# Position bias: the coefficient matrices written by GpSimd in quarters of partitions, and the first pair's operands loaded and split in the first groups

## Chip, cores and metric

The program runs on one core of one Trainium2 chip. The metric is the time of one execution in microseconds (us). The profile has one execution more, with its span (first to last instruction) beside its own time.

## The reference

Attention with a learned position bias feeds a chain of dense layers, and that feeds a top-1 mixture of 8 experts. Only the bias and the scores matter for this change:

```
B, H, S, D = 4, 8, 576, 64;  hidden = 32
rel = |i - j|;  psi_rel = log1p(rel);  psi_i = log1p(max(i, 1))
x    = psi_rel / psi_i                            # (S, S)
h    = relu(x * w1 + b1)                          # (S, S, 32)
bias = h @ w2                                     # (S, S, 8), one for each head
scores = q @ k.T / sqrt(D) + bias;  attn = softmax(scores);  out = attn @ v
x = (B*S, H*D) of out
x = ((x @ w1m) * (x @ w2m)) @ w3m @ w_out         # dense layers
result = top-1 of 8 experts, relu(x @ w1e) @ w2e, gated
```

## The kernel before

The program has four stages: `p0` (position bias, about the first 147 us), `p1` (attention, 16 pairs of a head and two batches), `p2` (dense layers) and `p3` (experts). An order of the instructions is written out by hand; each engine executes its own in that order, and so does the queue of the DMA issues on SyncE.

`p0` turns the bias into a matrix product. A hidden unit's relu of x is a step function of the row times something linear in log1p of the distance. The 576 distances are cut into 9 groups (`gg`) of 64; a group has 16 slots of 4 distances. The 128 partitions hold 4 distances x 32 hidden units. For each slot a mask of 128 x 576 is made (`mask`, L263 on VectorE, L261 on ScalarE): partition (distance g, unit u) and column i say if the unit is on in row i. The masks of group `gg + 1` are made while the matmuls of group `gg` run. For each group and each of up to five tiles `t` of rows (order 0, 4, 3, 1, 2; tile 4 has 64 rows) L345 multiplies the 16 masks by the matrix `mv`, 48 matmuls.

`mv` (two buffers, group `gg` uses `mvs[gg % 2]`) has the shape [128, 3, 16, 2, 8, 4]: three bf16 parts of a coefficient, slot, a = 0 for the linear or a = 1 for the constant coefficient, head, distance g. It is zero but where the partition's quarter (its 32 partitions) equals g. `split3` (L152, L154, GpSimd) cuts coefficients into three bf16 parts; `place` (L161, VectorE) multiplies them by the 0/1 matrix `bkb` of quarters and so writes zeros and values in one go, three operations of 128 x 512 elements. The constant coefficients (a = 1, `c3`) are placed once in each buffer, the linear ones (a = 0, from `coefs`) for each group. `coefs(gg + 2)` is called when group `gg` starts, and its `place` runs at the start of group `gg + 1`.

After a tile's matmuls `evac` scales one half of the result on ScalarE (L268) and adds the other on VectorE (L279, into `ds`). After each odd group `flush` writes the finished 128 distances to the DRAM tensor `dsym` (L221) and their mirror image, which GpSimd copies in reverse order into `md` (L235, three buffers), by L238. The attention stage reads the bias from `dsym` with `load_nb` (L382, L385).

In the same stage 24 blocks of weights are loaded as 64-bit floats (`load`, L180, five buffers) and converted (`begin`, `conv`: L89 on ScalarE, L91 to L93 on VectorE, L202 on ScalarE, L207 on VectorE), and products of these weights are made on TensorE (`wp_mm`, L245). The steps of a group are sorted by a key between 0 and 1 (`mixed`) and dealt out over its tiles. At each tile's end `ahead` takes a task of preparation for the attention stage from a list: `first` (constants, a clear, the loads of q, k and v of the first pair by L390, L391, L393), ten steps that split them (L403 to L423, on ScalarE and GpSimd), the loads of the second pair's q and k, and a small split of the gate weights. It does so from the fourth group on (`gg > 2`), not at a group's first tile.

Of the kernel before, what the change touches and what calls it, by code (L numbers as in the profile page):

```python
# [11 lines left out]
BF16 = mybir.dt.bfloat16  # L12
# [3 lines left out]
ALU = mybir.AluOpType  # L16
# [4 lines left out]
B, H, S, D = 4, 8, 576, 64  # L21
# [5 lines left out]
P = 128  # L27
# [43 lines left out]
class Kern:  # L71
# [4 lines left out]
    def T(self, pool, shape, dt, tag, **k):  # L76
        self.n += 1
        return pool.tile(shape, dt, name=f"{tag}_{self.n}", tag=tag, **k)
# [18 lines left out]
    def p0(self, dsym, wp_dram, late, ahead=lambda gg, ti: None):  # L97
# [3 lines left out]
        with ExitStack() as es:  # L101
# [14 lines left out]
            w1c, b1c, w2r = small[:, 0:1], small[:, 1:2], small[:, 2:2 + H]  # L116
            ivp, blk = ivb[:, 0:5], ivb[:, 5:9]
            mvs = [T(c, [P, 3, 16, 2, H, 4], BF16, f"mv{r}") for r in range(2)]
            th = T(c, [P, 144], F32, "th")
            tS = T(c, [P, 144], F32, "tS")  # L120
            sm = T(c, [P, 4], F32, "sm")
# [23 lines left out]

            def split3(src, n, sub):

                p3 = T(st, [P, 3, n, H], BF16, f"p3{sub}")
                rest = T(st, [P, n, H], F32, f"rest{sub}", bufs=1)
                for k in range(3):  # L150
                    v_ = src if k == 0 else rest
                    gp.tensor_scalar(out=p3[:, k], in0=v_, scalar1=1.0, scalar2=1.0, op0=ALU.mult, op1=ALU.mult)  # L152
                    if k < 2:
                        gp.tensor_tensor(out=rest, in0=v_, in1=p3[:, k], op=ALU.subtract)  # L154
                return p3

            def place(r, a, p3):

                src = p3 if p3.shape[2] == 16 else p3.to_broadcast([P, 3, 16, H])
                for k in range(3):  # L160
                    v.tensor_tensor(out=mvs[r][:, k, :, a], in0=src[:, k].unsqueeze(3).to_broadcast([P, 16, H, 4]),  # L161
                                    in1=bkb.unsqueeze(1).unsqueeze(1).to_broadcast([P, 16, H, 4]), op=ALU.mult)

            def coefs(gg):
                al = T(st, [P, 16, H], F32, "al", bufs=1)
                gp.tensor_tensor(
                    out=al, in0=cf[:, 0:1, :].to_broadcast([P, 16, H]),
                    in1=L4[:, 16 * gg:16 * gg + 16].unsqueeze(2).to_broadcast([P, 16, H]), op=ALU.mult)
                a3 = split3(al, 16, "a")
                return lambda: place(gg % 2, 0, a3)  # L170

            wf = T(late.xp, [P, KD * NT], F32R, "xT")
            woh, wol = (wf[:, KF * DM * n:KF * DM * (n + 1)].rearrange("p (k d) -> p k d", k=KF) for n in range(2))
# [2 lines left out]
            def load(i, b):  # L176
                raws[i, b] = T(st, [P, DM, 2], I32, "w3", bufs=NRAW)
                src = I["w_out"][:, 2 * i:2 * i + 2, :] if i < 4 else I["w3t"][i - 4]
                src = src.rearrange("p k d -> p (k d)")[:, DM * b:DM * b + DM]
                nc.sync.dma_start(out=raws[i, b].rearrange("p n t -> p (n t)"), in_=src.bitcast(I32))  # L180
# [103 lines left out]
            order = list(CV)  # L284
            for _ in range(NRAW):
                load(*order.pop(0))
            begin(0)
            c3 = split3(cf[:, 1:2, :], 1, "c")
            pl = coefs(0)
            for q in range(0, 16, 4):  # L290
                for k in range(3):
                    mask(0, q + k)
                mask(0, q + 3, True)
                if q == 0:
                    place(0, 1, c3)
                if q == 4:
                    pl()
            pl = coefs(1)
            prev = None
            st_ = {}  # L300
            for gg in range(9):
                ts = [t for t in (0, 4, 3, 1, 2) if 64 * gg < DMAX[t]]
                wph = list(range(WPH[gg], WPH[gg + 1]))
                bg, bga = [], []
                if gg < 8:
                    for q in range(16):
                        act = (q + 1) * NACT // 16 > q * NACT // 16
                        (bga if act else bg).append(lambda q=q, act=act: mask(gg + 1, q, act))

                cs = []  # L310
                n = CONV[gg + 1] - CONV[gg]
                for x, c_ in enumerate(range(CONV[gg], CONV[gg + 1])):

                    cs += [((x + 0.1 + 0.2 * k) / n, (c_, k)) for k in range(4)]
                    if c_:
                        cs.append(((x + 0.9) / n, (c_ - 1, 4)))
                if gg == 8:
                    cs.append((1, (len(CV) - 1, 4)))

                def cstep(n, k):  # L320
                    if k == 0:
                        begin(n + 1)
                        st_[n] = conv(*CV[n])
                    st_[n][k]()

                items = [(FM * (k + 0.5) / len(bg), x) for k, x in enumerate(bg)]
                items += [(k, lambda x=x: cstep(*x)) for k, x in cs]
                if gg < 8:
                    items.append((0, pl))
                    if gg == 0:  # L330
                        items.append((0, lambda: place(1, 1, c3)))
                    if gg < 7:
                        pl = coefs(gg + 2)
                mixed = [x for _, x in sorted(items, key=lambda x: x[0])]
                nt = len(ts)
                for ti, t in enumerate(ts):
                    for x in wph[len(wph) * ti // nt:len(wph) * (ti + 1) // nt]:
                        wp_mm(x // KF, x % KF)
                    n = 64 if t == 4 else P
                    pb = T(ps, [P, 2, 2, H, 8, 4], F32, "pb")  # L340
                    mv = mvs[gg % 2]
                    for s in range(16):
                        m_ = mss[gg, s // 8]
                        for k in range(3):
                            nc.tensor.matmul(out=pb[:n, s // 8, :, :, s % 8], lhsT=m_[:, s % 8, P * t:P * t + n], rhs=mv[:, k, s], start=(k == 0), stop=(k == 2))  # L345
                    fin = evac(*prev) if prev else None
                    for x in bga[len(bga) * ti // (nt - 1):len(bga) * (ti + 1) // (nt - 1)]:
                        x()
                    m0, m1 = len(mixed) * ti // nt, len(mixed) * (ti + 1) // nt
                    for x in mixed[m0:m1]:  # L350
                        x()
                    if fin:
                        fin()
                    ahead(gg, ti)
                    prev = (gg, t, pb)
# [1032 lines left out]
def build(tc, I, out):  # L1388
    K = Kern(tc, I, out)
    nc = tc.nc  # L1390
    with tc.manual_schedule(), ExitStack() as es:
# [18 lines left out]
            nc.gpsimd.memset(pre.qs[0].bitcast(F32), 0.0)  # L1410
            pre.load(0)

        tasks = [first, lambda: None] + [lambda x=x: x[0](*x[1:]) for x in pre.split(0)]
        tasks += [lambda: pre.load(1, v=False), lambda: wgs.append(K.wg_stack(c, cst["wg"]))]

        def ahead(gg, ti):
            if gg > 2 and ti and tasks:
                tasks.pop(0)()
            if ti == 1 and gg > 5:
                pre.load_nb(0, (8 - gg, ) if gg < 8 else (3,))  # L1420

# [120 lines left out]
```

## Time and profile before

| what | us |
|---|---|
| median of 3 runs | 1056.01 (1052.99 to 1056.57) |
| the profiled execution's own time | 1054.81 |
| its span | 1052.9 |
| TensorE busy | 979.5 (93%) |
| VectorE busy | 770.6 (73%) |
| ScalarE busy | 679.3 (65%) |
| GpSimd busy | 400.9 (38%) |

The shares are means over four stages that have different limits. For a change in the first stage, the busy times of that stage and the chain of waits in it say more. In the rows PE is TensorE's matmul, PEld its weight load, DVE VectorE, ACT ScalarE, POOL GpSimd, SPq the DMA queue of SyncE; L161 is line 161 of the kernel. PEclk is the share of full speed that TensorE's clock was granted.

### The profile page before, as it was taken

How to read it: one execution, taken by the hardware profiler on the slowest of the kernel's cores; microseconds unless marked ns; L12 is line 12 of the kernel's file. 1: busy time of each engine (PE TensorE's matmuls, PEld its weight loads, DVE VectorE, ACT ScalarE, POOL GpSimd, SP SyncE). 2: the span in 40 equal slices, each digit the busy share in tenths (PEclk: the TensorE clock that was granted, in tenths of full speed). 3: DMA queues.
4: the chain of work that ended last, by engine and by line, in shares of the span. 5: the costliest groups of instructions: out<-in, count | busy, mean ns of one | idle time of the engine just before them, and what ended most of it. 6: DMA issues, size and time to landing. Idle time of an engine off the chain costs nothing.

```text
span 1052.9 us, 21995 instructions
## 1 busy us (share of the span) xinstructions
PE 979.5 (93%) x8134; PEld 906.2 (86%) x8134; DVE 770.6 (73%) x1426; ACT 679.3 (65%) x1304; POOL 400.9 (38%) x468
## 2 busy tenths in 40 slices
PE   3588989999999999799999999999979999999996
PEld 3577778999999999699999999999978888888885
DVE  8997977999999998799321232123497999989996
ACT  5787758999999999344322222122226888888885
POOL 4255518899999986444100000000052121111111
PEclk9899989999999999889999999999989999999999
DMA  4599984453434422243000000000423326411173
GB/s 133 137 247 234 254 242 152 128 172 121 158 96 143 159 72 67 82 149 111 21 21 21 11 11 21 21 21 1 134 87 120 118 78 216 155 41 40 44 277 109
DMA packets 62419, 116.54 MB, mean 111 GB/s; under 512 B 14495, under 2 KB 33567, under 8 KB 62048
## 3 DMA queue, kind: packets, MB, share of 16 engines
q1 hardware_dynamic: 58496, 104.14, 32.0%
q0 software_dynamic: 3520, 10.75, 3.0%
q8 instruction: 67, 1.10, 0.4%
q14 instruction: 48, 0.39, 0.1%
q10 hardware_dynamic: 288, 0.15, 0.1%
HBM read 155.68 MB, written 25.15 MB: 172 GB/s over the span
## 4 chain that ended last, share of the span: by engine, by line
PE 43%; DVE 21%; issue 18%; DMA 12%; ACT 5%; POOL 0%; SPq 0%; POOLq 0%; DVEq 0%; ACTq 0%
PE ab L712 17%; DMA out<-or,sci 9%; PE o L781 8%; PE pv L569 6%; PE sc L485 4%; PE tr L541 3%; DVE etl L558 2%; DVE t L492 2%; DVE mv L161 2%; PE pv L245 2%; DVE mask L263 2%; DMA dsym<-ds 1%; ACT e L501 1%; DVE ds L279 1%; DVE qs L410 1%
## 5 line engine op out<-in xcount | busy, mean ns | idle before, releaser
L758 DVE TENSOR_TENSOR g<-ab,asb 128x256 f32<-128x256 f32 x72 | 30.4, 423 | 143.3 <-ACT asb L757 143.1
L512 POOL TENSOR_SCALAR e<-e,su 128x576 f32<-128x576 f32 x144 | 108.8, 760 | 27.2 <-DVE su L508 14.2
L492 DVE CUSTOM_DVE_ANT_0 t<-sc,nb 128x576 f32<-128x576 f32 x144 | 108.0, 750 | 11.4 <-PE sc L485 10.0
L501 ACT ACTIVATE e<-t,mn 128x576 f32<-128x576 f32 x144 | 112.2, 779 | 4.3 <-DVE mn L492 2.8
L558 DVE TENSOR_TENSOR etl<-tr,eth 128x512 fp32r<-128x512 f32 x144 | 98.9, 687 | 15.8 <-ACT eth L549 12.3
L345 PEld LDWEIGHTS <-mask 128*128 128x128 bf16 (+1 forms) x1872 | 67.1, 108 | 47.3 <-issue 36.2
L345 PE MATMUL pb<-mv,mask 128*128 128x64 bf16 (+1 forms) x1872 | 71.1, 203 | 38.8 <-DVE ds L279 22.2
L1328 POOL DMA_INDIRECT out<-or,sci x21 | 24.9, 1184 | 200.2 <-ACT or L1327 190.5
L485 PE MATMUL sc<-kh,qs 128*128 128x288 f32 x320 | 96.5, 318 | 3.3 <-DVE ds L279 3.3
L712 PE MATMUL ab<-xh,wh 128*128 128x256 f32 x576 | 95.6, 289 | 1.3 <-DVE g L758 1.3
L1225 DVE TENSOR_TENSOR w1l<-w1r,w1h 128x1024 fp32r<-128x1024 f32 x80 | 92.6, 1220 | 5.1 <-ACT w1h L1224 5.1
L541 PE MATMUL tr<-k_ident,e 128*128 128x128 f32 x576 | 86.4, 273 | 8.9 <-DVE etl L558 8.9
L1276 DVE TENSOR_TENSOR w2l<-w2r,w2h 128x1024 fp32r<-128x1024 f32 x80 | 92.6, 1220 | 2.7
L953 POOL DMA_INDIRECT xh<-x2r,gi x1 | 1.4, 1352 | 243.8 <-DMA w1r<-in_w1e 243.8
L712 PE MATMUL ab<-xh,wl 128*128 128x256 f32 x576 | 93.8, 286 | 0.0
L712 PE MATMUL ab<-xl,wh 128*128 128x256 f32 x576 | 93.8, 286 | 0.0
L485 PE MATMUL sc<-kl,qs 128*128 128x288 f32 x320 | 90.0, 297 | 0.0
L549 ACT CAST eth<-tr 128x512 fp32r<-128x512 f32 x144 | 82.6, 576 | 2.2 <-PE tr L541 1.4
L712 PEld LDWEIGHTS ab<-xh,wh 128*128 128x128 f32 x576 | 80.9, 195 | 1.7 <-DVE g L758 1.5
L1224 ACT CAST w1h<-w1r 128x1024 fp32r<-128x1024 f32 x84 | 82.1, 1069 | 0.0
L712 PEld LDWEIGHTS ab<-xh,wl 128*128 128x128 f32 x576 | 80.8, 195 | 0.0
L712 PEld LDWEIGHTS ab<-xl,wh 128*128 128x128 f32 x576 | 80.7, 194 | 0.0
(322 smaller groups left out, 2805.7 us busy)
## 6 DMA issues: line engine op xcount, KB each, us to landing
w1r<-in_w1e SPq DMA_DIRECT2D x84, 512.0 KB
w2r<-in_w2e SPq DMA_DIRECT2D x80, 512.0 KB
q<-in_qd SPq DMA_DIRECT2D x16, 576.0 KB
k<-in_kd SPq DMA_DIRECT2D x16, 576.0 KB
w<-in_w3t SPq DMA_DIRECT2D x16, 512.0 KB
raw<-in_w SPq DMA_DIRECT2D x16, 512.0 KB
nb<-dsym SPq DMA_DIRECT2D x7, 1152.0 KB
dsym<-ds SPq DMA_DIRECT2D x14, 512.0 KB
```

Of the source, the lines that this page charges most:

```text
L345: nc.tensor.matmul(out=pb[:n, s // 8, :, :, s % 8], lhsT=m_[:, s % 8, P * t:P * t + n], rhs=mv[:, k, s], start=(k == 0), stop=(k == 2))
L485: nc.tensor.matmul(out=sc[:, f, 0:288], lhsT=l, rhs=r, start=(n == 0), stop=(n == len(lst) - 1))
L492: nc.vector.tensor_tensor_reduce(out=t_.rearrange("p (f k) -> p f k", f=2), in0=sc[:, :, 0:288], in1=pre.nb[h % 2][:, tt, :].rearrange("p ...
L501: nc.scalar.activation(out=e, in_=t_, func=AF.Exp, scale=-1.0, bias=mn, accum_out=su[:, i % 3:i % 3 + 1])
L512: nc.gpsimd.tensor_scalar(out=e, in0=e, scalar1=su[:, i % 3:i % 3 + 1], scalar2=1.0, op0=ALU.mult, op1=ALU.mult)
L541: nc.tensor.transpose(pt[:, kb, :], e[:, P * kb:P * kb + P], ident)
L549: nc.scalar.copy(out=dh, in_=src)
L558: nc.vector.tensor_tensor(out=dl, in0=src, in1=dh.bitcast(F32), op=ALU.subtract)
L712: nc.tensor.matmul(out=p[:, a], lhsT=w[f][:, a, k, :], rhs=x[:, k, :], start=(k == 0 and n == 0), stop=(k == KD - 1 and n == 2))
L781: nc.tensor.matmul(out=o[:, a, 0:c1 - c0], lhsT=g[:, sl], rhs=w[:, f, c0:c1], start=(f == 0 and n == 0), stop=(f == KF - 1 and n == 2))
L1225: eng.tensor_tensor(out=w1l[:, k], in0=w1r[:, k], in1=w1h[:, k].bitcast(F32), op=ALU.subtract)
L1276: nc.vector.tensor_tensor(out=w2l[:, sl], in0=w2r[:, sl], in1=w2h[:, sl].bitcast(F32), op=ALU.subtract)
```

## The change

GpSimd clears both `mv` buffers once at the start. `place` then writes only the nonzero places: for each quarter g an operation on its 32 partitions copies the three parts of 16 slots x 8 heads (384 elements) to the places of that g. It does so on GpSimd, four operations for each group. Only the constant part of the first buffer stays on VectorE, in the old form. `coefs` splits and places in one call; `coefs(gg + 1)` stands at key 0.15 of group `gg`. The first group's masks are made ahead of the first conversion, 10 on VectorE and 6 on ScalarE (before 12 and 4). The list of preparation is cut in two: `first` and the split of the first pair are taken from the first group on, one task at each tile of the first group and two later; the loads of the second pair and the gate weights are taken from the fourth group on.

```diff
@@ -116,6 +116,8 @@
             w1c, b1c, w2r = small[:, 0:1], small[:, 1:2], small[:, 2:2 + H]
             ivp, blk = ivb[:, 0:5], ivb[:, 5:9]
             mvs = [T(c, [P, 3, 16, 2, H, 4], BF16, f"mv{r}") for r in range(2)]
+            for m_ in mvs:
+                nc.gpsimd.memset(m_, 0.0)
             th = T(c, [P, 144], F32, "th")
             tS = T(c, [P, 144], F32, "tS")
             sm = T(c, [P, 4], F32, "sm")
@@ -145,7 +147,7 @@
 
             def split3(src, n, sub):
 
-                p3 = T(st, [P, 3, n, H], BF16, f"p3{sub}")
+                p3 = T(st, [P, 3, n, H], BF16, f"p3{sub}", bufs=1)
                 rest = T(st, [P, n, H], F32, f"rest{sub}", bufs=1)
                 for k in range(3):
                     v_ = src if k == 0 else rest
@@ -156,18 +158,18 @@
 
             def place(r, a, p3):
 
-                src = p3 if p3.shape[2] == 16 else p3.to_broadcast([P, 3, 16, H])
-                for k in range(3):
-                    v.tensor_tensor(out=mvs[r][:, k, :, a], in0=src[:, k].unsqueeze(3).to_broadcast([P, 16, H, 4]),
-                                    in1=bkb.unsqueeze(1).unsqueeze(1).to_broadcast([P, 16, H, 4]), op=ALU.mult)
+                n = p3.shape[2]
+                for g in range(4):
+                    q = slice(32 * g, 32 * g + 32)
+                    src = p3[q] if n == 16 else p3[q].to_broadcast([32, 3, 16, H])
+                    gp.tensor_scalar(out=mvs[r][q, :, :, a, :, g], in0=src, scalar1=1.0, scalar2=1.0, op0=ALU.mult, op1=ALU.mult)
 
             def coefs(gg):
                 al = T(st, [P, 16, H], F32, "al", bufs=1)
                 gp.tensor_tensor(
                     out=al, in0=cf[:, 0:1, :].to_broadcast([P, 16, H]),
                     in1=L4[:, 16 * gg:16 * gg + 16].unsqueeze(2).to_broadcast([P, 16, H]), op=ALU.mult)
-                a3 = split3(al, 16, "a")
-                return lambda: place(gg % 2, 0, a3)
+                place(gg % 2, 0, split3(al, 16, "a"))
 
             wf = T(late.xp, [P, KD * NT], F32R, "xT")
             woh, wol = (wf[:, KF * DM * n:KF * DM * (n + 1)].rearrange("p (k d) -> p k d", k=KF) for n in range(2))
@@ -284,18 +286,16 @@
             order = list(CV)
             for _ in range(NRAW):
                 load(*order.pop(0))
+            c3 = split3(cf[:, 1:2, :], 1, "c")
+            coefs(0)
+            for q in range(16):
+                mask(0, q, q in (2, 5, 7, 10, 13, 15))
+                if q == 4:
+
+                    for k in range(3):
+                        v.tensor_tensor(out=mvs[0][:, k, :, 1], in0=c3[:, k].to_broadcast([P, 16, H]).unsqueeze(3).to_broadcast([P, 16, H, 4]),
+                                        in1=bkb.unsqueeze(1).unsqueeze(1).to_broadcast([P, 16, H, 4]), op=ALU.mult)
             begin(0)
-            c3 = split3(cf[:, 1:2, :], 1, "c")
-            pl = coefs(0)
-            for q in range(0, 16, 4):
-                for k in range(3):
-                    mask(0, q + k)
-                mask(0, q + 3, True)
-                if q == 0:
-                    place(0, 1, c3)
-                if q == 4:
-                    pl()
-            pl = coefs(1)
             prev = None
             st_ = {}
             for gg in range(9):
@@ -325,12 +325,11 @@
 
                 items = [(FM * (k + 0.5) / len(bg), x) for k, x in enumerate(bg)]
                 items += [(k, lambda x=x: cstep(*x)) for k, x in cs]
-                if gg < 8:
-                    items.append((0, pl))
-                    if gg == 0:
-                        items.append((0, lambda: place(1, 1, c3)))
-                    if gg < 7:
-                        pl = coefs(gg + 2)
+                if gg == 0:
+                    coefs(1)
+                    place(1, 1, c3)
+                elif gg < 8:
+                    items.append((0.15, lambda: coefs(gg + 1)))
                 mixed = [x for _, x in sorted(items, key=lambda x: x[0])]
                 nt = len(ts)
                 for ti, t in enumerate(ts):
@@ -1410,12 +1409,16 @@
             nc.gpsimd.memset(pre.qs[0].bitcast(F32), 0.0)
             pre.load(0)
 
-        tasks = [first, lambda: None] + [lambda x=x: x[0](*x[1:]) for x in pre.split(0)]
-        tasks += [lambda: pre.load(1, v=False), lambda: wgs.append(K.wg_stack(c, cst["wg"]))]
+
+        tasks = [first, lambda: None, lambda: None] + [lambda x=x: x[0](*x[1:]) for x in pre.split(0)]
+        tasks2 = [lambda: pre.load(1, v=False), lambda: wgs.append(K.wg_stack(c, cst["wg"]))]
 
         def ahead(gg, ti):
-            if gg > 2 and ti and tasks:
-                tasks.pop(0)()
+            for _ in range(2 if gg else 1):
+                if tasks:
+                    tasks.pop(0)()
+            if gg > 2 and tasks2:
+                tasks2.pop(0)()
             if ti == 1 and gg > 5:
                 pre.load_nb(0, (8 - gg, ) if gg < 8 else (3,))
 
```

## Rows read from the trace of the kernel before

**Rows 1.** Chain of waits to 147 us: by line; a piece (start, length, what).

```profile
by line: DVE mv L161 14.1%; DVE mask L263 12.3%; DMA dsym<-ds 10.6%; DVE ds L279 10.1%; issue 9.3%; DVE w3ta L92 7.7%; PE pb L345 5.7%; DVE w3ta L91 4.9%; PE pv L245 3.8%; DMA q<-in_qd 3.7%; DVE w3ta L93 3.4%; DVE xT L207 3.4%; DVE w3l L207
...
56.05 10.79 DMA dsym<-ds
```

**Rows 2.** By stretch: length, each engine's busy us (count), clock, DMA share, GB/s.

```profile
core 0: us, PE busy (x) PEld busy (x) DVE busy (x) ACT busy (x) POOL busy (x), PEclk, DMA share, GB/s
0.00:13.30 13.30, 0.42 (x2) 0.31 (x3) 9.53 (x27) 8.21 (x11) 7.40 (x23) 1.00 0.63 215
13.30:35.50 22.20, 14.03 (x287) 13.21 (x286) 21.96 (x43) 12.86 (x22) 5.45 (x11) 0.85 0.32 98
35.50:53.70 18.20, 9.71 (x240) 9.47 (x241) 18.03 (x32) 13.56 (x23) 5.58 (x6) 0.81 0.55 127
53.70:67.70 14.00, 11.00 (x250) 9.92 (x249) 11.89 (x24) 13.14 (x22) 7.17 (x9) 0.88 1.09 278
67.70:84.80 17.10, 13.92 (x272) 11.80 (x272) 13.21 (x24) 10.73 (x18) 7.88 (x11) 0.99 0.87 243
84.80:100.60 15.80, 15.20 (x265) 12.84 (x263) 14.20 (x28) 12.59 (x21) 8.74 (x12) 0.90 0.91 226
100.60:117.40 16.80, 15.11 (x270) 12.45 (x270) 16.80 (x22) 13.06 (x24) 15.79 (x20) 1.00 0.98 246
117.40:131.00 13.60, 12.72 (x220) 10.60 (x219) 13.50 (x29) 10.19 (x20) 2.31 (x4) 1.00 0.95 232
131.00:142.00 11.00, 11.00 (x172) 9.21 (x171) 10.90 (x25) 7.41 (x16) 0.00 (x0) 1.00 0.93 243
...
147.00:1052.90 905.90, 874.63 (x6118) 814.78 (x6118) 636.42 (x1174) 574.75 (x1130) 339.41 (x373) 0.98 0.29 95
```

**Rows 3.** L161 alone, by stretch, and its sum.

```profile
13.30:35.50 22.20, 4.35 (x7) 0.85 0.32 98
...
100.60:117.40 16.80, 6.60 (x6) 1.00 0.98 246
...
sum 147.00, DVE 26.02; mean DVE 2.60
```

**Rows 4.** L161: ns min/median/max, first and last start; L263 in two stretches.

```profile
L161 DVE TENSOR_TENSOR mv<-p3a,bkb x27: 674/684/1912, 11.2 to 130.6; 128x512 bf16<-128x512 bf16 x27
...
35.50:53.70 18.20, 3.07 (x7) 0.81 0.55 127
...
100.60:117.40 16.80, 5.08 (x7) 1.00 0.98 246
```

**Rows 5.** GpSimd to 147 us by line: busy us, mean ns, idle before.

```profile
L235 POOL TENSOR_SCALAR md<-ds 128x512 f32<-128x512 f32 x16 | 13.0, 826 | 46.6 <-DVE ds L279 27.5 <-DVE mask L263 12.0 <-DMA dsym<-md 7.0
L152 POOL TENSOR_SCALAR p3a<-resta 128x128 bf16<-128x128 f32 x18 | 8.0, 442 | 1.6
...
L413 POOL TENSOR_TENSOR kl<-k,kh 128x576 fp32r<-128x576 f32 x2 | 3.7, 1856 | 0.2
L410 POOL TENSOR_TENSOR qs<-q,qs 64x576 fp32r<-64x576 f32 x2 | 2.8, 1419 | 0.2
L403 POOL TENSOR_SCALAR kh<-k 128x576 fp32r<-128x576 f32 x2 | 2.5, 1248 | 0.0
L235 POOL TENSOR_SCALAR md<-ds 64x512 f32<-64x512 f32 x2 | 2.2, 1101 | 3.4 <-DMA dsym<-md 2.3 <-DVE ds L279 1.1
...
L1410 POOL MEMSET qs<- 128x1280 f32 x1 | 1.2, 1168 | 0.0
```

**Rows 6.** Timeline at the start: start us, length us, operation, idle before.

```profile
7.27 0.30 POOL L152 TENSOR_SCALAR p3a<-resta 128x128 bf16<-128x128 f32 x1
...
13.34 7.44 PE L345 MATMUL pb<-mv,mask 128*128 128x64 bf16 x142 [0.39 <-DVE mv L161]
```

**Rows 7.** Timeline from 78.5 to 92 us: two waits.

```profile
81.93 0.67 ACT L406 CAST qs<-q 128x576 fp32r<-128x576 f32 x1 [4.63 <-DMA q<-in_qd]
...
91.35 1.01 POOL L235 TENSOR_SCALAR md<-ds 128x512 f32<-128x512 f32 x1 [12.03 <-DVE mask L263]
```

## The prediction

> **What bounds the kernel now.** The change touches the first stage alone, the one that builds the position bias, so I first asked how long that stage is and what ends it. The chain of waits up to 147 us [rows 1] names VectorE lines for most of its length; the largest single line is L161, the operation that the change takes away, with 14.1% of 147 us, 20.7 us. What is not VectorE there is a wait for a bias write to land (10.8 us from 56.05 us on), some TensorE and a load of q. Then I cut the stage at the first matmul of a group's second tile (the 64-row tile), which comes once in each group [rows 2]. The reader is to see, line by line, VectorE's busy time against the length, and then the engine that is next behind it: in the second and third lines VectorE is busy 21.96 of 22.2 and 18.03 of 18.2 us, and nothing else comes near; from 53.7 us on ScalarE (13.14 of 14.0) or TensorE (15.20 of 15.8, 12.72 of 13.6, 11.00 of 11.0) stands directly behind or in front of it. The DMA share is 0.32 and 0.55 in those two early lines and 0.87 to 1.09 after them. After 147 us TensorE is busy 874.6 of 905.9 us: nothing of the change runs there, so I let the rest of the program keep its length and move as a block.
>
> **What VectorE loses.** L161 runs 33 times, 26.02 us [rows 3]. Three of them stay (the constant part of the first matrix), 30 go to GpSimd: 30 x 26.02/33 = 23.7 us. The first group's masks go from 12 on VectorE and 4 on ScalarE to 10 and 6; two masks at 0.44 us (3.07 us for 7 [rows 4]) are another 0.9 us. So VectorE loses 24.6 us of work; ScalarE gains two masks ahead of the first matmul, where it waits anyway.
>
> **What GpSimd gains.** For each of 9 groups four quarter operations (32 partitions x 384 elements), and four more for the constant part of the second matrix: 40. None of this shape is in the trace. The number of partitions does not seem to shorten an operation: the 64-partition copies of L235 took 1.10 us, the 128-partition ones 0.83 [rows 5]. Below, the 128-element conversion (0.44 us); above, that 64-partition copy of 512 elements (1.10 us). I take a value between the 128- and the 512-element row by element count, 0.44 + 2/3 x (0.83 - 0.44) = 0.70 us: 28 us in all, 2.8 us in each group (bounds 18 and 44 us). Two clears of 12 KB in all come first; the clear of 5 KB took 1.17 us, so 2.8 us, or 5.6 us if the cost goes by elements and not by bytes. They start while nothing else can run, since GpSimd's first real operation waits for a load until about 3 us, and end at 3 to 6 us.
>
> **The start.** GpSimd now has the first coefficients split at 7.57 us; the matmuls start in earnest at 13.34 us, when VectorE has placed them [rows 6]. With the clears the split comes at 7.6 to 10.5, the four quarters add 2.8: 10.4 to 13.3 us. VectorE in the meantime has 10 masks and 3 placements. So the start is nothing to 3 us earlier; should VectorE's placement wait for GpSimd's write into the same matrix, 2 us later. I take zero.
>
> **What of the 24.6 us is left, stretch by stretch** [rows 2, 3]. I take VectorE's placements off, then ask which engine is next.
>
> 13.3 to 35.5: 21.96 less 4.35 is 17.6, ScalarE 12.9, TensorE 14.0. GpSimd's extra work beside it slows some VectorE operations; I add 1.2 us. Gain 3.4.
>
> 35.5 to 53.7: most of the first pair's split comes here, out of later groups. GpSimd's L413, L410 and L403 alone are 9.0 us [rows 5], and the v operations come on top. VectorE: 18.0 less three placements at the median of 0.684 us [rows 4], 15.9, plus 1.6 for that company. Gain 0.5.
>
> 53.7 to 67.7: ScalarE's 13.14 of 14.0 is the floor. Gain 0.3.
>
> 67.7 to 84.8: here ScalarE stood 4.63 us before the conversion of q, waiting for its load, and VectorE after it [rows 7]. The load now goes out right behind the first five weight loads, when the DMA share is 0.32, so this wait goes; what is late next is TensorE, 13.92. Of 3.2 us I take 2.0, because the second pair's load moves into this group (from the seventh) and the bias writes still share the queue with it.
>
> 84.8 to 100.6: TensorE 15.20. Gain 0.3.
>
> 100.6 to 117.4: six placements took 6.60 us beside the split; both go, and TensorE's 15.11 remains. Of 1.7 I take 1.2.
>
> 117.4 to 131: VectorE 13.5 less 2.1, TensorE 12.72. Gain 0.6 of 0.9.
>
> From 131 on: TensorE is full, then the last bias write has to land. Nothing.
>
> Sum: 3.4 + 0.5 + 0.3 + 2.0 + 0.3 + 1.2 + 0.6 = 8.3 us, of the 14.2 us that the floors would allow (4.6 + 2.3 + 0.9 + 3.2 + 0.6 + 1.7 + 0.9). From it I take 1 us for GpSimd being late once (first rival). 7.3 us less than the profiled execution's 1054.8 is 1047.5; that execution lies 1.2 us under the median of the runs, which I leave as it is.
>
> **The price of company on VectorE.** In 100.6 to 117.4 GpSimd was busy 15.79 us. The six placements took 6.60 us where the median of 0.684 gives 4.1, and the seven masks 5.08 us where those from 35.5 us on took 3.07 [rows 3, 4]: 4.5 us lost to 15.79 us of GpSimd, 0.29 us each. For 28 us that would be 8.1 us; but over half of that loss fell on the placements themselves, which are gone. Zero to 8.1, and I take 2.8 in the two early stretches, where VectorE sets the pace.
>
> A rule of the Trainium skill speaks against the change. GPSIMD Engine Reference, section Engine selection, says to keep elementwise work on VectorE, and its section Specifications that GpSimd shares its SBUF interfaces with VectorE and contends with some of its modes. The row above agrees that there is a price; what it would be if it were full is the third rival.
>
> **Rivals.**
>
> *GpSimd's order, not its speed.* The coefficients of a group were split two groups ahead and placed by VectorE; now splitting and placing stand in GpSimd's queue within the group before, behind the mirrored copies of L235. One of these waited 12.03 us for its turn [rows 7], and whatever is queued behind it waits too: the next matrix, and with it the next group's first matmul. For: in 35.5 to 53.7 GpSimd has 5.6 us now, and with the split (some 12) and the quarters (2.8) over 20 in 18 us; the rest falls in front of the fourth group's matrix. Against: 53.7 to 67.7 has 14.0 - 7.2 - 2.8 = 4 us of room. Cost 3 to 5 us of the 7.3: 1050 to 1053.
>
> *Nothing to see: the DMA paces.* From 53.7 on the DMA share is 0.87 to 1.09. If the bias writes and weight loads can't go faster, VectorE's time turns into waits at line 279 and at the weights. For: the 10.8 us of the chain. Against: 1.5 MB of q, k and v (128 x 2 x 576 x 4 bytes twice and 0.33 MB) leave this stretch, 6 us at its 240 GB/s, and the second pair's load only moves within it. The early gain would be held up and given back: 1053 to 1056.
>
> *Company takes it all.* If every microsecond of GpSimd took one from VectorE, 28 us would come back against 24.6: 3 us longer, 1058. For: placements of up to 1.9 us in [rows 4]. Against: 0.29 us for each in the busiest stretch, and the operations that suffered most there are the ones that go.
>
> *Slower: GpSimd sets the pace.* Its place is every group from the second on: GpSimd has 7 to 9 us now in a stretch of 14 to 17; with four quarters of p us it needs 8 + 4p. At p = 2 it equals the 16 us of such a group; at 2.5 each of seven groups grows by 2 us and the time is 1069. The rows say 0.44 to 1.10 with a full row of contention, against it; the writes leave gaps of three elements, which no row has, speak for it.
>
> *More.* If the floors were reached everywhere, 14.2 us: 1041.
>
> **How the numbers follow.** Forecast (1043 to 1050) 0.55; GpSimd's order 0.17; DMA paces 0.11; company takes it all 0.04; GpSimd's speed 0.09; more than the forecast 0.04. A change under 0.3% (3.2 us, so 1052.8 to 1059.2) can't be told from none here. Faster is 0.55 + 0.04 + nearly all of 0.17: 0.74; same 0.17; slower 0.09. Leaving out GpSimd's speed, the full price of company and the tail of more (0.17), the range is 1042 to 1056.
>
> **What would show it.** Right: L161 with 3 operations; no wait of ScalarE for q in this stage; the first group ends some 3 us earlier and the first score matmul comes at about 140 us instead of 147; quarters of 0.5 to 1 us. Wrong: TensorE's pb matmuls waiting for GpSimd; quarters over 1.5 us; VectorE still busy 99% up to 53.7 us with masks near 0.7 us; or a stage that ends early while the attention behind it starts no sooner, because the bias has not landed.

## The result: 1.4% slower, and where 17 us went

The changed kernel takes 1068.81 us (median of 4 runs, 1067.76 to 1070.88) against 1055.26 for the kernel before (4 runs, 1052.99 to 1056.57): ratio 1.0137 [1.0118, 1.0155]. The forecast of 1047.5 was wrong in sign, and the time lies outside its range (1042 to 1056). The profiled execution took 1070.88 us with a span of 1069.1 and a mean granted clock of 0.972; it is the longest of its four, and its span is 16.2 us longer than that of before where the medians differ by 13.6.

The first score matmul now starts at 164.05 us instead of 147.09. What follows it is 905.1 us long, and it was 905.9 [rows 2], so everything to be explained lies in the first stage: 17.0 us. This is the table of stretches of the changed kernel, cut at the same marks as [rows 2]; the line numbers have moved (the quarters are L165, VectorE's three remaining placements L296, masks L265, mirrored copies L237, L279 is L281, the bias matmul L344).

```profile
core 0: us, PE busy (x) PEld busy (x) DVE busy (x) ACT busy (x) POOL busy (x), PEclk, DMA share, GB/s
0.00:15.90 15.90, 0.01 (x1) 0.12 (x2) 12.51 (x24) 9.42 (x13) 14.05 (x22) 1.00 0.77 280
15.90:40.60 24.70, 15.33 (x288) 14.66 (x287) 24.46 (x35) 13.50 (x23) 21.61 (x25) 0.72 0.29 89
40.60:61.80 21.20, 9.81 (x240) 9.55 (x241) 21.03 (x29) 14.55 (x24) 14.13 (x15) 0.78 0.56 134
61.80:87.90 26.10, 13.09 (x250) 11.98 (x250) 16.59 (x29) 14.54 (x24) 15.97 (x26) 0.72 0.88 233
87.90:101.20 13.30, 13.30 (x265) 11.23 (x264) 11.77 (x22) 10.90 (x19) 4.40 (x5) 1.00 0.80 181
101.20:121.70 20.50, 15.79 (x269) 13.39 (x268) 13.88 (x24) 13.96 (x23) 14.26 (x22) 0.92 0.81 218
121.70:136.40 14.70, 14.70 (x271) 12.38 (x270) 9.16 (x17) 8.86 (x16) 8.37 (x12) 1.00 0.67 174
136.40:149.00 12.60, 12.60 (x221) 10.54 (x220) 12.53 (x20) 10.25 (x21) 11.75 (x14) 1.00 0.77 185
149.00:160.00 11.00, 11.00 (x172) 9.19 (x172) 10.86 (x23) 7.17 (x15) 0.51 (x1) 1.00 0.86 210
164.00:1069.10 905.10, 871.85 (x6118) 811.42 (x6118) 637.24 (x1174) 574.35 (x1130) 339.49 (x373) 0.99 0.29 95
```

Line by line against [rows 2], with the gain that the prediction gave each stretch (from the last 64-row tile to the first score matmul it is 4.05 us against 5.09). These are differences of two single profiles, so the large ones count, not one of a microsecond:

```
stretch of before      forecast gain   measured
  0    to  13.3             0            -2.6
 13.3  to  35.5            +3.4          -2.5
 35.5  to  53.7            +0.5          -3.0
 53.7  to  67.7            +0.3         -12.1
 67.7  to  84.8            +2.0          +3.8
 84.8  to 100.6            +0.3          -4.7
100.6  to 117.4            +1.2          +2.1
117.4  to 131.0            +0.6          +1.0
131.0  to 147.1             0            +1.0
```

Three places lose: the start, the two stretches where VectorE is busy 24.46 of 24.7 and 21.03 of 21.2 us as before, and two later stretches (26.1 and 20.5 us) in which no engine is near full. From 87.9 us on TensorE is busy all of every stretch but the one of 20.5, as forecast.

What fills the 26.1 us is told by the chain of waits to 164 us (line shares, then its two longest pieces: start, length, what) and by the list of waits to 170 us (us in total, times, longest):

```profile
by line: DMA dsym<-md 17.6%; PE pv L247 14.5%; PE pb L344 14.0%; issue 9.0%; DVE mask L265 6.8%; POOL mv L165 6.7%; POOL md L237 4.9%; DVE w3ta L92 3.1%; DVE ds L281 3.0%; DVE w3ta L91 2.7%; DVE xT L209 2.3%; POOL p3a L154 1.7%; DVE bkb L13
...
65.06 9.85 DMA dsym<-md
94.54 7.59 DMA dsym<-md
```

```profile
PE pb L344 <- POOL mv L165: 32.4, 3, 15.9
POOL md L237 <- DMA dsym<-md: 22.1, 5, 8.3
...
DVE ds L281 <- ACT tmp L270: 20.4, 7, 7.9
ACT tmp L270 <- PE pb L344: 18.1, 6, 10.6
```

VectorE has given up the head of the chain of [rows 1]: bias writes lead it, then TensorE's own lines, and GpSimd's quarters stand in it with 6.7%. The timeline of the fourth group shows one turn of this (start, length, operation, idle time before it and what ended it):

```profile
75.05 0.62 POOL L237 TENSOR_SCALAR md<-ds 128x512 f32<-128x512 f32 x1 [8.30 <-DMA dsym<-md]
75.64 0.46 POOL L169 TENSOR_TENSOR al<-cf,L 128x128 f32<-128x128 f32 x1
...
79.25 4.15 POOL L165 TENSOR_SCALAR mv<-p3a 32x384 bf16<-32x384 bf16 x4
83.45 2.72 PE L344 MATMUL pb<-mv,mask 128*128 128x64 bf16 x48 [11.77 <-POOL mv L165]
...
86.20 0.69 ACT L270 ACTIVATE tmp<-pb,ivb 128x512 f32<-128x512 f32 x1 [10.62 <-PE pb L344]
```

Read it from the top. The mirrored copy (L237) needs one of three buffers (ScalarE's copies of the weight products, L251, take turns in the same three), the buffer is free when an earlier bias write has landed, and GpSimd stands 8.30 us for that; it is the write that stands in the chain above from 65.06 us on, for 9.85 us. The next group's coefficients (L169) are queued behind this copy although they wait for nothing. They start at 75.64 and the quarters end at 83.4, TensorE has stood 11.77 us, and ScalarE behind it 10.62.

The quarters, by line on GpSimd to 170 us (busy us, mean ns, idle before), with the clears:

```profile
L165 POOL TENSOR_SCALAR mv<-p3a 32x384 bf16<-32x384 bf16 x36 | 38.8, 1079 | 7.9 <-PE pb L344 5.6
L120 POOL MEMSET mv<- 128x3072 bf16 x2 | 5.3, 2672 | 0.3 <-POOLq L1538 0.3
L165 POOL TENSOR_SCALAR mv<-p3c 32x384 bf16<-32x384 bf16 x4 | 4.3, 1076 | 0.3
```

Forty quarters are 43.1 us, where I had put 28. Beside them VectorE slows down. These are its lines from 15.9 to 61.8 us:

```profile
L265 DVE TENSOR_SCALAR mask<-qi,th 128x576 bf16<-128x576 f16 x19 | 13.2, 717 | 0.0
L93 DVE SCALAR_TENSOR_TENSOR w3ta<-w,w3ta 128x512 int32<-128x512 int32 x9 | 9.9, 1098 | 0.2
...
L281 DVE TENSOR_TENSOR ds<-pb,tmp 128x512 f32<-128x512 f32 x7 | 4.7, 677 | 0.0
```

The same three lines before, from 13.3 to 53.7 us:

```profile
L263 DVE TENSOR_SCALAR mask<-qi,th 128x576 bf16<-128x576 f16 x20 | 8.2, 442 | 0.0
L93 DVE SCALAR_TENSOR_TENSOR w3ta<-w,w3ta 128x512 int32<-128x512 int32 x9 | 6.8, 753 | 0.2
...
L279 DVE TENSOR_TENSOR ds<-pb,tmp 128x512 f32<-128x512 f32 x7 | 4.8, 683 | 0.0
```

The operation that reads PSUM (L279, now L281) keeps its time, the others grow. In all, VectorE's work there without L161 was 33.8 us (39.99 [rows 2] less 6.20 for 10 placements) in 64 operations; now it is 45.49 us in 63: 11.7 us more, beside 24.7 us more of GpSimd (35.74 against 11.03).

The start, from the timeline to 45 us:

```profile
0.73 5.28 POOL L120 MEMSET mv<- 128x3072 bf16 x2 [0.29 <-POOLq L1538]
3.46 2.58 DVE L130 CAST bkb<-ivb 128x4 bf16<-128x4 f32 x1
...
11.18 4.66 POOL L165 TENSOR_SCALAR mv<-p3a 32x384 bf16<-32x384 bf16 x4
15.89 7.16 PE L344 MATMUL pb<-mv,mask 128*128 128x64 bf16 x144 [15.89 <-POOL mv L165]
```

The clears end at 6.01 us. VectorE's cast of 4 elements, 0.17 us before, lasts until then (3.46 + 2.58 = 6.04). GpSimd's own first coefficient operation stands behind the clears: it starts at 6.13 us, before at 3.05.

### The profile page after: what moved, and what is told of

Read it like the earlier page. It is cut to its first block, busy times and chain, and to the rows that moved or that the text cites. A ratio compares the mean times of both kernels' runs of the same rounds, so it can differ in the third digit from the quotient of the medians.

```text
span 1069.1 us, 21991 instructions
## 1 busy us (share of the span) xinstructions
PE 979.2 (92%) x8134; PEld 906.0 (85%) x8134; DVE 773.4 (72%) x1394; ACT 680.2 (64%) x1306; POOL 445.7 (42%) x510
## 4 chain that ended last, share of the span: by engine, by line
PE 45%; issue 18%; DVE 16%; DMA 13%; ACT 4%; POOL 3%; POOLq 0%; ACTq 0%; DVEq 0%
PE ab L711 17%; DMA out<-or,sci 9%; PE o L780 8%; PE pv L568 6%; PE sc L484 4%; PE tr L540 3%; PE pv L247 3%; DMA dsym<-md 3%; DVE etl L557 2%; PE pb L344 2%; DVE t L491 2%; ACT e L500 1%; DVE qs L409 1%; DMA raw<-in_w 1%; DVE mask L265 1%
## 5 line engine op out<-in xcount | busy, mean ns | idle before, releaser
L344 PE MATMUL pb<-mv,mask 128*128 128x64 bf16 (+1 forms) x1872 | 73.7, 206 | 54.4 <-POOL mv L165 32.4
L344 PEld LDWEIGHTS <-mask 128*128 128x128 bf16 (+1 forms) x1872 | 69.9, 111 | 62.5 <-issue 44.0
L511 POOL TENSOR_SCALAR e<-e,su 128x576 f32<-128x576 f32 x144 | 108.7, 761 | 27.2 <-DVE su L507 15.9
L711 PE MATMUL ab<-xl,wh 128*128 128x256 f32 x576 | 92.9, 284 | 0.0
L1223 ACT CAST w1h<-w1r 128x1024 fp32r<-128x1024 f32 x84 | 82.1, 1069 | 0.0
L540 PEld LDWEIGHTS tr<-k_ident,e 128*128 128x128 f32 x576 | 69.4, 140 | 13.2 <-issue 12.5
```

The costliest lines, as they stand in the source:

```text
L511: nc.gpsimd.tensor_scalar(out=e, in0=e, scalar1=su[:, i % 3:i % 3 + 1], scalar2=1.0, op0=ALU.mult, op1=ALU.mult)
L540: nc.tensor.transpose(pt[:, kb, :], e[:, P * kb:P * kb + P], ident)
L711: nc.tensor.matmul(out=p[:, a], lhsT=w[f][:, a, k, :], rhs=x[:, k, :], start=(k == 0 and n == 0), stop=(k == KD - 1 and n == 2))
```

## Experiments

The experiments ran on other chips, on which the kernel before took 1059.4 to 1060.2 us; each ratio is to the kernel before on its own chip and is the number to compare. "Order" below is the theory that the quarters stand in the wrong place in GpSimd's queue; its rivals are "preparation" (the early load and split of the first pair crowd GpSimd and VectorE) and "speed" (the quarter operation itself is too slow).

**One half of the change each** (place_only, tasks_only). The first kernel has the new placement with the old list of preparations, the second the old placement with the new list.

```diff
 place_only (the changed kernel, old list)
-        tasks = [first, lambda: None, lambda: None] + [... pre.split(0)]
-        tasks2 = [lambda: pre.load(1, v=False), ...]
+        tasks = [first, lambda: None] + [... pre.split(0)]
+        tasks += [lambda: pre.load(1, v=False), ...]
-            for _ in range(2 if gg else 1): ...
+            if gg > 2 and ti and tasks:
 tasks_only (the kernel before, new list): the same lines the other way
```

> The changed kernel with the old list of preparation (first pair's loads and split back in the fourth to seventh group); GpSimd still writes the matrices. Theory 'order' (the next group's matrix waits in GpSimd's queue behind mirrored copies that wait for their bias writes): the copies before the fourth group remain, so most of the loss remains, 1061 to 1067 us, and the first matmul of the fourth group still waits 5 us or more for L165. Rival 'preparation' (the early split fills GpSimd in the first groups, and that is what comes late): 1054 to 1058 us and no such wait.

> The kernel before with the new list of preparation alone; VectorE places as before. Theory 'order': nothing on the path of the matrices waits for the mirrored copies, and ScalarE's wait for q (4.6 us) goes: 1049 to 1055 us. Rival 'preparation': the early split delays the mirrored copies and with them the bias writes: 1059 us or more.

place_only: 1.0214 [1.0195, 1.0232], 21 us more, above what either theory had; its first matmul of the fourth group waits 14.45 us for L165. tasks_only: 0.9969 [0.9953, 0.9986], 3.3 us less. Preparation falls as a cause: the moved load and split help on both sides here, and the placement alone loses more than the whole change. In tasks_only the wait of ScalarE for q [rows 7] is gone.

**The order alone** (coefs_first). The coefficients go to the head of the group's list of work, ahead of the mirrored copies.

```diff
-                    items.append((0.15, lambda: coefs(gg + 1)))
+                    items.append((0.0, lambda: coefs(gg + 1)))
```

> The changed kernel with the next group's coefficients at key 0 in place of 0.15, which puts them in GpSimd's queue ahead of the last tile's mirrored copies. Theory 'order': the wait of 11.8 us at the fourth group's first matmul falls to 4 us or less, that at the sixth too; 1057 to 1061 us. Rival 'speed' (quarter operations of 1.08 us and the operations of VectorE that they slow make the loss, wherever they stand): 1066 to 1069 us.

1.0028 [1.0014, 1.0043]: 3 us above before instead of 14. Its timeline at the fourth group:

```profile
66.30 0.40 POOL L169 TENSOR_TENSOR al<-cf,L 128x128 f32<-128x128 f32 x1
...
70.44 4.84 POOL L165 TENSOR_SCALAR mv<-p3a 32x384 bf16<-32x384 bf16 x4
...
75.33 0.91 PE L344 MATMUL pb<-mv,mask 128*128 128x64 bf16 x14 [5.02 <-POOL mv L165]
75.36 0.89 POOL L237 TENSOR_SCALAR md<-ds 128x512 f32<-128x512 f32 x1
```

The copy now stands behind the quarters, and TensorE's wait is 5.02 us instead of 11.77 (I had expected 4 or less); the sixth group's, 4.7 us in the changed kernel, is gone. Order is shown as the larger part. What is left is no wait for a write: from 54.8 to 75.3 us GpSimd is busy 19.33 of 20.5 us, with copies and the first pair's split, and from 66.30 us on with this group's split and quarters.

**The clears** (clear_f32). The same bytes, cleared as 1536 words of 4 bytes instead of 3072 of 2.

```diff
-                nc.gpsimd.memset(m_, 0.0)
+                nc.gpsimd.memset(m_.bitcast(F32), 0.0)
```

> The changed kernel with the two clears written as 1536 words of 4 bytes for each partition in place of 3072 of 2. If the clear costs by elements, the two take 2.7 us in place of 5.3, VectorE's small operations at the start are no longer held up, and the first matmul comes 2.4 us earlier: 1066 to 1067 us. If a later wait takes it up, 1068 to 1069 us.

On GpSimd, by line:

```profile
L120 POOL MEMSET mv<- 128x1536 f32 x2 | 2.7, 1380 | 0.3 <-POOLq L1538 0.3
```

Half the time, and the first matmul comes at 13.41 us instead of 15.89. The whole is 1.0108 [1.0091, 1.0125]; that interval overlaps the change's own, so only the start is shown. The next kernel, first_f32, has this edit and coefs_first's; the kernel before was profiled again beside it.

> Key 0 for the coefficients and clears by words, together. Theory 'order and start' (the queue order costs 11 us, the clears 2.5, and the rest of the change gains and loses about the same): within 2 us of the kernel before. Rival 'speed': still 3 us or more above it.

> The kernel before, for a profile on the chip of the other runs of this call. Nothing is told apart: its first stage ends within 3 us of the 147 us seen.

first_f32: 1.0016 [1.0001, 1.0032], as 'order and start' had it. Against clear_f32, on the same chip, only the key differs: 1.0108 has become 1.0016, 9.7 us. The kernel before has its first score matmul at 152.89 us on this chip, where the first profile had 147.09 on the other: 5.8 us apart, where 3 were expected. Whether the chip makes that or the one execution, two profiles do not tell; stage times are compared within one chip only.

**What makes a quarter slow** (dense_write). The change writes each value 8 bytes behind the last. Here the 384 values of a quarter go side by side, on first_f32.

```diff
-   out=mvs[r][q, :, :, a, :, g]
+   out=mvs[r][q] ... [:, 384 * a:384 * a + 384]
```

> As first_f32, but each quarter operation writes its 384 elements side by side instead of 8 bytes apart (they land in wrong places, so the result is not the bias). If the gaps make the quarter operation slow, it falls from 1.03 us to 0.5 to 0.6, GpSimd loses 18 us and the time 3 to 6 us against first_f32. If the bf16 input or the small number of partitions makes it slow, it stays at 1 us and so does the time.

The whole took 1066.48 us, 1.0079 [1.0055, 1.0103], 5 us more than first_f32 instead of less. But with a wrong bias the later stages do other work (6178 matmuls behind the first score matmul, 6118 in first_f32, and 11 us more), so only the first stage is read: the first score matmul comes at 146.72 us against 153.75 in first_f32. The quarters in both (ns min/median/max), dense_write first:

```profile
L165 POOL TENSOR_SCALAR mv<-p3a x36: 500/509/1129, 8.1 to 125.0; 32x384 bf16<-32x384 bf16 x36
```

```profile
L165 POOL TENSOR_SCALAR mv<-p3a x36: 998/1096/1557, 8.7 to 137.8; 32x384 bf16<-32x384 bf16 x36
```

The gaps cost half of the operation; with them gone the stage is 7 us shorter, 2.3 of them ahead of the first matmul. Speed is a cause beside order; heads_psum below shows it with a right bias.

**Placing on ScalarE** (act_place). tasks_only with four scaled copies on 128 partitions, which needs no cleared matrix.

```diff
-                for k in range(3): v.tensor_tensor(out=mvs[r][:, k, :, a], ...)
+                for g in range(4):
+                    nc.scalar.activation(out=mvs[r][:, :, :, a, :, g], in_=src, func=AF.Copy, scale=blk[:, g:g + 1])
```

> The kernel before with the new list of preparation, and the matrices placed by ScalarE: four copies of 384 elements on all 128 partitions for each group, each scaled by a column of the 0/1 matrix, no clear. Theory 'company' (GpSimd's work on the matrices slows VectorE, ScalarE's would not): VectorE's masks stay near 0.4 us and VectorE loses 24 us; ScalarE gains 22 to 28 us and becomes the limit in the early groups: 2 to 8 us under the kernel before. Rival: ScalarE, whose tmp copies VectorE waits for, sets the pace at once: 2 us or more above it.

1.0045 [1.0030, 1.0059], 4.8 us more; the rival had it for the time, 'company' for VectorE: its masks take 439 ns in the first 60 us. There ScalarE (fourth busy column) is now the busiest engine:

```profile
0.00:60.00 60.00, 25.29 (x528) 24.38 (x529) 41.86 (x83) 50.63 (x75) 23.62 (x47) 0.80 0.51 149
```

**The same bias with side-by-side writes** (heads_inner). The heads are stored innermost, so that a quarter writes runs of 8 values, one for each head. The matmul's output is permuted back on its way into PSUM; VectorE's three placements follow the new order, and key and clears are first_f32's.

```diff
-            mvs = [T(c, [P, 3, 16, 2, H, 4], BF16, ...)]
+            mvs = [T(c, [P, 3, 16, 2, 4, H], BF16, ...)]
-                    gp.tensor_scalar(out=mvs[r][q, :, :, a, :, g], ...)
+                    gp.tensor_scalar(out=mvs[r][q, :, :, a, g], ...)
-  matmul(out=pb[:n, s // 8, :, :, s % 8], ...)
+  matmul(out=pb[:n, s // 8, :, :, s % 8].rearrange("p a h g -> p a g h"), ...)
```

> first_f32 with the matrix stored with the heads innermost, so that a quarter operation writes runs of 8 heads (16 bytes) and not single values 8 bytes apart; the matmul writes its result in the permuted order. Theory 'gaps' (the single values make a quarter operation twice as long, and VectorE waits for the shared side as long): quarters 0.5 to 0.6 us, first stage 6 us shorter than first_f32's, 3 to 6 us under the kernel before. Rival: runs of 16 bytes are as slow as single values, or TensorE's permuted writes cost as much: within 2 us of first_f32, so 0 to 3 us above the kernel before.

1.0126 [1.0105, 1.0146], some 12 us worse than first_f32: the quarters fell to a median of 512 ns, but 48 matmuls went from 1.57 to 2.85 us and TensorE was busy 40.00 of the 40 us from 60 to 100.

```profile
93.24 2.85 PE L344 MATMUL pb<-mv,mask 128*128 128x64 bf16 x48
```

Three variants of it: the key back at 0.15 (heads_late); the old list of preparations (heads_oldprep); each quarter issued twice (heads_twice).

> heads_inner with the coefficients back at key 0.15, as in the changed kernel. If the order in GpSimd's queue is a price of its own (a wait for a bias write to land, which fast quarters do not shorten), it costs 7 to 11 us against heads_inner; if it only shows because the quarters are slow, 0 to 4 us.

> heads_inner with the old list of preparation. place_only stood 7 us above the changed kernel, tasks_only 4 us under the kernel before; if the early loads and split are worth that here too: 3 to 7 us above heads_inner. If they only helped around the slow quarters: within 2 us.

> heads_inner with each quarter operation issued twice, so 40 more on GpSimd (about 20 us), same result. Theory 'company': VectorE's masks grow again and the time by 5 to 8 us. Rival (only the order counts, GpSimd has room): 0 to 3 us.

heads_late 1.0213 [1.0196, 1.0230], 9 us above heads_inner: order again. heads_oldprep 1.0086 [1.0068, 1.0103], 4 us under it, where I had expected more time or none: by the profiles the early split costs 4.8 us in the stretch up to the third group's 64-row tile (20.6 us, 15.8 without it) and saves 3.4 in the next (17.4, 20.8 without it). heads_twice 1.0180 [1.0163, 1.0197]: 40 more quarters cost 5.9 us, within what 'company' had. But VectorE's masks did not grow (634 ns in heads_inner from 16.0 to 52.7 us, 636 in the same stretches here). By the profiles 2.6 us come at the first matmul, which waits for the doubled quarters, the rest up to the fourth group; from there on TensorE is busy all the time, and the next 92.9 us keep their length. So this run shows a price of GpSimd's time in the early groups, and not that it is company.

What was still open was whether fast quarters can be had without slow matmuls. Two ways: PSUM itself in the new order, so that both sides run straight and only the reads of PSUM (L270, L281) jump; or the new order in the matrix alone, with TensorE reading it in steps of 16 bytes.

```diff
 heads_psum
-                    pb = T(ps, [P, 2, 2, H, 8, 4], F32, "pb")
+                    pb = T(ps, [P, 2, 2, 8, 4, H], F32, "pb")
+  matmul(out=pb[:n, s // 8, :, s % 8], ...)
-  in_=pb[:n, :, 0].rearrange("p b h s g -> p b h (s g)")
+  in_=pb[:n, :, 0].rearrange("p b s g h -> p b h (s g)")
 heads_read
+  matmul(..., rhs=mv[:, k, s].rearrange("p a g h -> p a h g"))
```

Both are heads_inner in the rest; in heads_psum VectorE's read in L281 changes like ScalarE's, and in heads_read the matmul writes PSUM in the old order.

> Heads innermost in the matrix and in the partial result too, so TensorE writes runs of 32; ScalarE and VectorE read the partial result with a stride of 8 values in L270 and L281. Theory 'gaps': matmuls at 1.5 us for 48 again, quarters 0.5 us, first stage 6 us shorter than first_f32's; 3 to 6 us under the kernel before. Rival: the strided reads take longer than 0.68 us each (78 of them) and the gain goes: 0 to 4 us above it.

> Heads innermost in the matrix only, and the matmul reads it in the old order (stride of 16 bytes). If TensorE reads 2-byte values at such a stride at full rate: as heads_psum, 3 to 6 us under the kernel before. If not: its 48 matmuls take near 3 us as in heads_inner, 10 us or more above.

heads_read: 1.1260 [1.1242, 1.1278]; 48 matmuls take 5.59 us. heads_psum: **0.9945 [0.9930, 0.9960]**, 1054.23 us against 1060.09: 5.8 us less, faster than both kernels. Its matmuls, its quarters, and ScalarE's and VectorE's reads of PSUM (ns min/median/max):

```profile
88.06 1.57 PE L344 MATMUL pb<-mv,mask 128*128 128x64 bf16 x48
```

```profile
L165 POOL TENSOR_SCALAR mv<-p3a x36: 502/592/1057, 8.7 to 123.9; 32x384 bf16<-32x384 bf16 x36
...
L270 ACT ACTIVATE tmp<-pb,ivb x39: 663/683/706, 15.7 to 140.1; 128x512 f32<-128x512 f32 x30, 64x512 f32<-64x512 f32 x9
L281 DVE TENSOR_TENSOR ds<-pb,tmp x39: 668/678/692, 19.1 to 146.5; 128x512 f32<-128x512 f32 x30, 64x512 f32<-64x512 f32 x9
```

Reading PSUM in jumps costs nothing that shows (a mean of 677 ns for L281 in the changed kernel). Last, heads_psum with the key at 0.15 (heads_psum_late), and with the old list of preparations (heads_psum_old):

> heads_psum with the coefficients at key 0.15. If the queue order is a price of its own: 6 to 11 us above heads_psum, as heads_late was 9 us above heads_inner. If it needs slow quarters: 0 to 4 us.

> heads_psum with the old list of preparation. If the early loads and split still pay (tasks_only was 4 us under the kernel before): 2 to 6 us above heads_psum. If their company for VectorE in the first two groups costs as much as they bring: within 2 us.

heads_psum_late 0.9993 [0.9982, 1.0004], 5.1 us above heads_psum, between the two forecasts: order has a price of its own, and slow quarters raise it. heads_psum_old 0.9959 [0.9944, 0.9973], not to be told from heads_psum. With clear_f32 and first_f32 this fills a square, in us to the kernel before (ratio less 1, times 1060; the left column is from one chip, the right from another):

```
                          quarters with gaps    side by side
coefficients at 0.15           +11.4               -0.7
coefficients at 0.0             +1.7               -5.8
```

Order costs 9.7 us with slow quarters and 5.1 with fast ones; the gaps cost 12.1 with the late order and 7.5 with the early one. The two do not simply add up (4.6 us, with some 3 us of noise). That a slow quarter lengthens the queue that the late order stands in would explain it; no run shows that.

## Why the prediction was wrong, step by step

**The step that failed** is "From it I take 1 us for GpSimd being late once (first rival)", with the "4 us of room" that the rival's "against" found in the stretch from 53.7 us. I took GpSimd's length less its busy time for room. It was not: part of that idle time is GpSimd standing at a mirrored copy until a bias write lands (22.1 us in five waits in the changed kernel), and nothing behind the copy in GpSimd's queue can use it. [rows 7] showed such a stall of 12.03 us, and I named it in the rival, but priced the rival at 3 to 5 us. (That row names a mask as what ended the wait, which no copy reads. By the trace's semaphores the copy also waited for the write issued at 81.44 us, which landed at 91.18; the copy started at 91.35.) The forecast for that stretch was +0.3 us and it lost 12.1; for the one of 20.5 it was +0.3 too, and it lost 4.7. These two make 17.4 of the 25.3 us between the sum of 8.3 and the measured -17.0. Moving one key took 9.7 us off the whole on one chip (clear_f32 to first_f32, 1.0108 to 1.0016), and about 11 by ratios from two chips (1.0137 to 1.0028), which shows the cause.

**The quarter's duration** was mis-sized: 0.70 us taken, 1.08 measured, at the upper bound of 1.10. Interpolating by element count left out the gaps that the last rival named; the runs show them as half of the operation (0.51 against 1.10 us medians). That rival's own mechanism, p = 2 to 2.5 us in every group, did not come: of the eight stretches behind the start four keep their length or get shorter. That its 1069 us is the measured time is luck.

**Company on VectorE** was mis-sized too: 2.8 us taken, 11.7 measured in the first two of these stretches, 0.47 us for each us that GpSimd worked more, instead of 0.29. So of the 6.2 us of placements taken from VectorE there nothing showed: the forecast +3.4 and +0.5 became -2.5 and -3.0. I had discounted the row of 0.29 because over half of that loss fell on the placements; masks and L93 suffer as well, as the rows of before and after show. The rule of the Trainium skill that I weighed there (GPSIMD Engine Reference, section Specifications, shared SBUF interfaces) agrees with these rows: L93, with two inputs in SBUF, grew from 753 to 1098 ns, and L281, with one of its two in PSUM, did not grow. The 0.47 is no rate, since heads_twice added GpSimd work and the masks stayed as they were. The rival "company takes it all" was right for these two stretches and wrong for the whole: the largest loss was a queue.

**The start** was taken as zero, at most 2 us later if VectorE's placement waited for GpSimd; it cost 2.6 us another way. The clears took 5.28 us (5.6 had been named, if the cost goes by elements), and the first four quarters 4.66 instead of 2.8.

**Right**: L161 on VectorE is down to 3 operations; the wait for q is gone and that stretch gave 3.8 us (2.0 taken); TensorE is the floor from 87.9 us on but for the stretch of 20.5; the rest of the program moves as a block; DMA does not pace by itself, since order alone gave back 9.7 us with the same transfers. Two of the signs of being wrong came as written: "TensorE's pb matmuls waiting for GpSimd", and VectorE busy 99% of the early stretches with masks of 0.7 us. With the order and the gaps both mended the change is worth 5.8 us (heads_psum); the new list of preparations by itself, with VectorE placing, is worth 3.3 (tasks_only), and the intervals of the two overlap.

Not tried: more buffers for the mirrored copies, and a third coefficient matrix. Whether the 5 us that TensorE still waits at the fourth group in coefs_first would go with either stays open.

## What to carry to other kernels

Idle time on an engine is room only for work that stands in front of the wait: before moving work to an engine, find the instructions there that stop for a buffer, and put what another engine needs soon ahead of them. Price an elementwise operation on GpSimd by how its output lies in memory, not by its elements alone; a change of the layout on the far side (here PSUM, whose jumping reads showed no cost) can make the writes run straight. On VectorE, busy all the time in the early groups here, work taken away counted only after subtracting what the operations left lost beside a busier GpSimd.

## What the runs showed of the hardware

- A GpSimd write of 32 x 384 2-byte values took 0.51 us side by side (dense_write) and 1.10 us with 8 bytes from one value to the next (first_f32; medians).
- A GpSimd clear of 128 x 3072 2-byte values took 2.67 us; the same bytes as 1536 4-byte words took 1.38 us.
- Beside a busier GpSimd, VectorE's masks went from 442 to 717 ns and L93 from 753 to 1098, while L281 with an operand in PSUM stayed at 677; a 4-element cast was held 2.58 us, to the end of a clear.
- 48 matmuls of 64 columns took 1.57 us (heads_psum); with the PSUM output permuted 2.85 us (heads_inner), with the moving operand read in steps of 16 bytes 5.59 us (heads_read). ScalarE's and VectorE's f32 reads of PSUM kept their 0.68 us when each value came to lie 8 behind the last.
